# A smaller leading tile, uneven triple tiles, and weight sums spread over PSUM and GpSimd in a two-convolution transducer kernel

## The chip, the cores and the metric

The kernel runs on one core of one Trainium2 chip. The metric is the device time of one execution in microseconds (us), lower is better. Engines are written as the profile writes them: PE is TensorE (PEld its weight loads), DVE is VectorE, ACT is ScalarE, POOL is GpSimd, SP is SyncE, which issues the DMAs here.

## The reference

```
x (2, 4000, 512), w1, w2 (5, 512, 512), g (2, 8, 512), w_f, w_g, w_o (512, 512), all bf16
h  = gelu(conv(x, w1, 5 taps, pad 2))[:, ::2]        # (2, 2000, 512)
f  = gelu(conv(h, w2, 5 taps, pad 2))[:, ::2]        # (2, 1000, 512)
fe = f @ w_f ;  ge = g @ w_g                         # (2, 1000, 512), (2, 8, 512)
j  = tanh(fe[:, :, None, :] + ge[:, None, :, :])     # (2, 1000, 8, 512)
out = j @ w_o                                        # (2, 1000, 8, 512)
```

The convolutions contract 512 channels for each of 5 taps; only every second output is kept, so only those are computed.

## The kernel before, in words

**Order.** A class `Plan` records every operation once, and a table `ORDER` holds, for each engine, the written-out sequence in which that engine gets its operations (each pair of characters is the number of one operation in the order of recording). Semaphore waits are added from the cells that operations read and write. An engine works strictly in its sequence: when its next operation waits, everything behind it waits too. Helpers (`memset`, `tt` for a tensor_tensor, `stt` for a scalar_tensor_tensor, `act` for an activation, `mm` for a matmul over four slices of 128 channels) record the operations, so most of the profile's rows carry the line of a helper: L398 is `tt`, L404 `act`, L412 `mm`.

**The start.** DVE sets a tile `zero` (L419). PE runs eight warming matmuls of 512 columns on it (`warm_mm`, L480 to L486). POOL makes the identity from it (L422). The first rows of x come straight by two DMAs (`load_xr`, 128 rows and 78 rows). PE transposes them in 32 steps against the identity (`turn`, L489), 16 for each load, and ACT and DVE copy the turned rows from PSUM to `xs[0]` (DVE: L505). The taps of w1 come in the order 0, 4, 2, 1, 3 on SP (`load_w1`): taps 0 and 4 in two halves each.

**The leading tile.** The first 408 outputs of h (2 x `NA`, `NA` = 204) of the first batch are computed tap by tap: `direct`, 5 taps x 4 slices of channels x 4 blocks of outputs, 80 matmuls of 408 columns, taps in the order 0, 4, 2, 1, 3.

**The triple tiles.** The other outputs of both convolutions come in `Triple` tiles, where nine matrix products do the work of fifteen. A tile has six phases of x (every sixth row, turned by a transposing DMA on SP: `load_xq` into `xq0`, `xq1`, later `xp2`, `xp0`; phases in the order 4, 0, 2, 1, 3, 5). ACT and DVE form sums and differences of phases in steps (`step`: d0 to d2 scale by 2, r0 to r2, t2, tm, sm and so on), written to `row0` and `row1` or back over a phase. For each of four blocks m of outputs a `Unit` runs products over these: t2 first into a PSUM bank, ACT keeps 1.5 times the result (`sd`), then tm and sm on top of it, ACT keeps its negative, then t1 and s1, and DVE adds (`acc<-acc,sd`). The rest of the first batch is covered by two tiles of `N3` = 266 and 266 columns, the second batch and the second convolution by tiles of 334.

**The weight sums.** The products need sums of taps: `w1part(m)`, for each block m of 128 outputs. With t = w0 + w4: v = t - w2 (a third of it goes to `w1_x[0]`), u = 4 w4 + w0 + 2 w2 (a third goes to `w1_x[1]`), and t + w2 goes to `w1_t[2]`. From taps 1 and 3: 2 w1 (`w1_t[1]`), w1 + w3 (`w1_t[0]`), w1 - w3 (`w1_x[2]`). DVE makes the sums in SBUF buffers (`ssum`, fp32), ACT the scaled copies.

**Later stages.** fe and the joint output use products over sums as well (`Feature`, `Seven`): sums of tanh outputs (`ss<-jT`, L903, on DVE and POOL), evictions of PSUM (`sn<-acc`, L834 on ACT and L835 on DVE), sums over these (`og<-acc,sn`) and stores. These come in the same number before and after; the table `ORDER` says which engine does which.

Of the kernel before, what the change touches and what calls it, by code (L numbers as in the profile page):

```python
# [8 lines left out]
ALU = mybir.AluOpType  # L9
# [54 lines left out]
class Op:  # L64
# [6 lines left out]
        "0Y0Z0a0b0c0d0e0f0g0i0k0l0n0q0y0z0_0-101112131415161718191A1B1C1D1E1F1G1H1p2L2l321I1J2v2S2T1r1s2w2n2N2o2O34352y2V2z2W"  # L71
        "3F3G3C3D392s3X2t3A3Y3Q3S3g3T403a3b3q4A3n3i3r3j3d4J423e4T4B434U3o473t4L4j4M4D3u484E4h4W4Q4k4R5U4X4u4r4x4s4o524z4p4_4v"
        "5e55565y535f586667595W5X5b5c6U5_6W5h6e6X5-6f6u6h6i6364695i6-726b6c6w6A736x707H7a7J7K7y7R7k7O7l7S7h7U7P757V7i7c867d7_"
        "7-767n8c8C897o8A8M87838N8J848e8K8f8E8F8v8_8w8m8n989990918j8P958k8Q9B8x8y9M9O8p9P8q9T9U969Z9a9c9C9o9x9d9W9z9X9qA5ACA2"
        "ABA4A99sAWAGAI9tArAsANAKB3B4BAAiAQAjATBBARAUBMAlAmBeBNAoApBfBtAyAzBGBhBiA-BTBUB0BDBHBEBJCABzBaBKBbBWBXCBBkBlCQCHB_CI"
        "CNBnC0COC1BqBoCKBrCLCuCcC6CdCRCfCvCgCTCjCkC7CxCyCUDODSDBDCDTC_DeDEC-DFCnCoD1DVD2DWDfDYDKDZDlDoDLDpDmDwE1E2D4E4E5D5Db"
        "DcDxDsDtENE7E8EOEKEDEEEiEAEjEBELEcEXEYEdF7ETEoFLEUF0EfElFMEgF1F8FXEmFDFOFfF3FBFPFgFsF4F_G4F-FRFiG5FZFjFSFUFVG1G2GNGG"
        "GHGTGUFoFpFuGAGWG7G8GZGXGJGKGOGaGnGoGcGqGrGhGfHCGwGxH0GdHEH3H1HVH4H9HWHAHbHhH6I4I5HKHNHcHLH7HOHjHpHqHeHYHZHfHRHSIAI7"
        "I8IKHyHzHsIhIbIBILHtIcIiIDJ4J5INIOIRIeISIEIkJKIrIsIfJAJBIlJLJDI_J7IuIvJXI-J8JdJaJbJYJEJgJeJRJNJhK0K1JnJoJSJqJwJOKGK6"
        "JrK3K4KHKbJxK7KVKWK9KcKAKYKZL0KeKfKlKmKNL1KOKJKuL6KKKoL7LZKpL3LTL9KvLGLULaLHLALcL4LyLNLsLjLOLkLtLzLdLJLKLWM2LXM3MCMR"  # L80
        "L-M0MSMuMDMvLmLnM5MJM6MhMiMKMFMUMXMGMVMYMaMxMyMbM_N1M-NPN8N9MoMkNQMpN2MlNBNCNFNGNSNTNYNuNvO1ONNZOONfNgNiNjNVNWN_O2Nx"
        "NyN-O8OdNmOeNnO9OwOTOWOUOxOqOrOXOBOQOCOtOROFOkOuOGP4OzP5OgPBPCOlOhP7O_PHPIPKP8PLPiQ9PjPQPRPNPOQAPXPYPaPrPoPpPbPsPlPm"
        "PyPePfPzQMP-Q0Q3Q4QNQCQDQIQJQFQGQPQQQTQUQXQYQbQeQfQi"),
    "act": (
        "080h0m1U0r1x1W1a1z1Z251Y2b1q271K2m1L2M1-1j2U1t2x1l1M1O332d2R1N3E2g2f2X2u2_3Z3B3H3R2h3h413c2r3K3s3M4K3x3f4C4V3p3y3w38"
        "494F4b3m3W3v4i5V5D464t4Y4P4S4y4d5C574q4w5z5B4n6E5A5g5154685d6V6g786j6v6G6M6a5j65795S6B5a745T627I7A7b6d7s5x7z7T717N6_"
        "7W7j7m5q6T7Q5w778D8d7u7g828O8B886s6t7p6S8X8-8L858o8Y9A8W9G8I8R8i8l9N7G948r9I976m9b9V9D9e9S8z9p9_9rA69YAcAXA8AFAtAdAP"
        "AfAMAeAhASAnBOAVB8BuB9AgBgCFCECs9wB7CGCqB-CJC2CCCrCDCeCwChDQCtDPDRFJDDD-CpE0DGDgEaDnFHCXEbE3D6FxFFFGFID_FwEMEFEZEPGS"
        "FyEpFNF2FYFKG_FCF5FhFzIWFkG-GIGVFvI0IVJ2GpGRGgGsHDJVH2J_HXI2IYHMHPI6I1IXIaJ-IMICIjJ6IdJ3ItI3IZJMIwJWJZK_JfK2JpKTJsNN"
        "KILSKdKRK-KnL2KUKyKqLwL8LVLILRLlL_NqKSLxM4MTMEMwMtMjMHKzMQNsN0MPMmNDNLNRMsOPNhNwNXNkNtNMOfOMNOODNrOpP6OLOiPJOoP9PPPZ"  # L90
        "PkQBPcPqP_Q1QOQHQRQgQdQk"),
    "dve": (
        "000j0o0p1R1S1v1T1V1X231w1u212Z1_1y24221b2a261d1c1Q1e1g1f1P1h1i1k28202p1m2P2Y362c1n2Q2q372e1o302i2k2j2-3U3I3V313J3L3k"
        "3P3z3l3O3N4H3-444I3_4N454Z4l4G4m4a4O4c4-4f4e504g5m5E5G5F5k5Y6D6J6F6C5l5Z5P6Y6l6L6K6Z605Q615N5O5t5p6I7C6H7D7Y6y7B5R5u"
        "6z7L7M7Z6P7q5o7X6Q5r7E6k5s5v7r7e6N806O7t7f6R816p7v6n7w6o6q7x6r8G7F8H8b8g8Z8h8u928t939H8a9F9h9f9Q9l9j9R9g8s9k9J9E9i9n"
        "9y9K9-A09mADA3A7AAA1AEAJ9uAHAOAL9vB5B69LAkAYAZBPAbAuBQAvBCAqA_BjBVBIBFBvB1BYBcBmBLByCaBpCMCPBsCZClC8CzCbCVDUCSD0CWD8"
        "DkDXEyEGEzEHD3DqDMDaE6DdDyDuEqDzEtErGCE9EkECEeEvFbEwEVEhEnFEF9FQExGjFtG6G0FTFaFWG3FqGBG9GYGLGbGPGiHHIGHlHIGyGeHFH5Hi"
        "HBHdH8HkHrHaHgHTI9H_HuIHIoJGIPIFITIgJHIpImJCJ9J0JcJFJjKDJkJiJPJTK5JyKXK8KBKaKgKPKLKjKkLDM8KwLbLfM9L5LBLPLuLYLLM1LeLo"
        "M7MAMBMdN4MLMZMWMzNAMqMcNHNUN3OZNdNbO4NcO5NaO3NzNoOAOVO0OsOSOyOvOHOmPDOYO-PMP2PTPuP3PUPvPSPnPgPtQ5QEQKQVQZQcQj"),
    "pool": (  # L100
        "01020304050s0t0u2A0v0w0x295n8VAaBSAwBRAxBwCYDjBxD9D7DhDiE-DAE_EJEsEIFcEuFeGkFdGlGDHGGFGEHmIIGmHoHJHnJIInIqIJJJKCJlKF"
        "KhKEJmLCKiLFLgLELiLhMfMeN5MgN6N7NeO6O7OaOcObP0P1PWPVPwPx"),
    "sp": (
        "0607090A0B0C0D0E0F0G0H0I0J0K0L0M0N0O0P0Q0R0S0T0U0V0W0X2B2C2D2E2F2G2H2I2J2K5H5I5J5K5L5M8S8T8UB2BZBdC3C4C5C9CiCmDHDIDJ"
        "DNDrDvEQERESEWF6FAFlFmFnFrGMGQGtGuGvGzHQHUHvHwHxH-IQIUIxIyIzJ1JQJUJtJuJvJzKMKQKrKsKtKxLMLQLpLqLrLvMIMMMNMOMnMrNENINJ"
        "NKNlNpOEOIOJOKOjOnPAPEPFPGPdPhQ2Q6Q7Q8QLQSQWQaQh"),
# [3 lines left out]
class Plan:  # L110
# [25 lines left out]
    def dma(self, eng, fn, reads=(), writes=(), sem=None, nbytes=524288, rate=320e3):  # L136

        o = Op()
        o.eng, o.fn, o.dma, o.signal, o.idx, o.alt, o.port = eng, fn, True, False, len(self.ops), None, False
        o.reads, o.writes, o.cost, o.pin, o.after, o.wire = tuple(reads), tuple(writes), 0.43, True, [], nbytes / rate  # L140
# [144 lines left out]
def bass_standalone__seq2seq_rnn_t_joint__speech_kernel(  # L285
# [25 lines left out]
    NA, N3 = 204, (266, 266)  # L311
# [9 lines left out]
    with ExitStack() as es:  # L321
# [27 lines left out]
        zero = at("zero", [NT], BF16)  # L349
# [5 lines left out]
        xq = [Buf(nc, f"xq{i}", [6, NK, (288, 288)[i]], BF16, v.end - v.bytes) for i, v in enumerate((xs[1], w2_sb))]  # L355
# [52 lines left out]
        def mm(o, pairs, start, stop, check=True):  # L408
# [9 lines left out]
        zv = zero[:]  # L418
        pl.op("dve", lambda e: e.memset(zv.ap, 0.0), (), (zv,))  # L419
# [3 lines left out]
            out=idv.ap, in_=zero[0:P].ap, compare_op=ALU.not_equal, fill=1.0, base=0,  # L423
            pattern=[[-1, P]], channel_multiplier=1), (zero[0:P],), (idv,))
# [15 lines left out]
        def load_x6(buf, b, ph, j0, col, n=336):  # L440
# [4 lines left out]
            return pl.dma("sp", lambda e: e.dma_start_transpose(out=dst.ap, in_=src), (), (dst,), nbytes=n * 2 * D, rate=172e3)  # L445
# [18 lines left out]
        def load_xq(i, ph):  # L464
            o = load_x6(xq[i], 0, ph, 2 * NA // 3 + i * N3[0] - 2, 0, -(-(N3[i] + 3 - i) // 16) * 16)
            if (i, ph) in ((0, 4), (0, 0)):
                o.wire = 1.050 if ph else 2.520
# [768 lines left out]
```

## Time and profile before

| | us |
|---|---|
| device time, median of 3 runs | 248.95 |
| lowest and highest run | 248.75, 248.99 |
| span of the profiled execution, on its one core | 247.2 |
| median of the runs less that span | 1.75 |

| engine | busy us | share of the span | instructions |
|---|---|---|---|
| PE (matmul) | 242.8 | 98% | 1932 |
| PEld (weight load) | 186.1 | 75% | 1932 |
| DVE | 224.8 | 91% | 403 |
| ACT | 210.7 | 85% | 359 |
| POOL | 83.8 | 34% | 90 |

The profile lists the profiled execution by its span alone: from its first instruction to its last. What the device time holds beyond it, some 1.75 us, lies around the program. Times in the profile's rows count from the start of the span. A row of the timeline gives start, length, engine, line, operation and tiles, and in brackets how long the engine was idle and what released it; a run of equal instructions stands as one row with its count, and its length reaches to the end of the last one, which for matmuls is modelled and overlaps the next row. Starts are therefore what the pace is read from.

### The profile page before, as it was taken

Reading aid. Unit: us, or ns where it says so; the run is one execution under the profiler, and the core shown is the slowest. Engines: PE = TensorE matmul, PEld = TensorE weight load, DVE = VectorE, ACT = ScalarE, POOL = GpSimd, SP = SyncE. Lnnn points to the kernel's source line nnn. Section 1 sums busy time; section 2 is a strip of 40 time slices with the busy share of each in tenths; the row PEclk is TensorE's granted clock in tenths of the full one; section 3 lists DMA queues with packets and bytes.
Section 4 is the critical chain, followed back from the end, with each engine's and each line's share of the span. In section 5 each row is a group of like instructions: output and inputs, shape, how many; then the busy total and the mean of one; then the engine's idle time right before and its main releaser. Section 6 shows DMA issues by size and latency. Waiting matters only on the chain.

```text
span 247.2 us, 5277 instructions
## 1 busy us (share of the span) xinstructions
PE 242.8 (98%) x1932; PEld 186.1 (75%) x1932; DVE 224.8 (91%) x403; ACT 210.7 (85%) x359; POOL 83.8 (34%) x90
## 2 busy tenths in 40 slices
PE   8999999999999999999999999999999999999995
PEld 4657888877666666666567888778788888888883
DVE  1799998867999999699998999999999999999994
ACT  3269799899669857986799999999999999999992
POOL 1000000000000000000015584677887886796861
PEclk9999999999999999999999999999999999999999
DMA  6998999997700340000000234413433655356377
GB/s 215 331 193 168 185 157 205 150 177 174 254 2 3 119 135 3 1 1 3 0 0 3 85 102 139 143 48 129 131 127 103 195 171 172 132 187 200 123 258 233
DMA packets 57890, 31.87 MB, mean 129 GB/s; under 512 B 33835, under 2 KB 57659, under 8 KB 57865
## 3 DMA queue, kind: packets, MB, share of 16 engines
q1 hardware_dynamic: 57577, 31.41, 48.5%
q8 instruction: 15, 0.25, 0.4%
q10 hardware_dynamic: 288, 0.13, 0.2%
q14 instruction: 10, 0.08, 0.1%
HBM read 7.66 MB, written 16.38 MB: 97 GB/s over the span
## 4 chain that ended last, share of the span: by engine, by line
PE 98%; DVE 0%; issue 0%
PE acc L412 97%; PE acc L496 1%; DVE ost L835 0%; DVE xs L505 0%; DVE zero L419 0%
## 5 line engine op out<-in xcount | busy, mean ns | idle before, releaser
L398 DVE TENSOR_TENSOR og<-acc,sn 128x512 bf16<-128x512 f32 x93 | 60.0, 690 | 1.9 <-PE acc L412 1.2
L412 PE MATMUL acc<-tw,ss 128*128 128x256 f16 x372 | 58.0, 273 | 0.0
L404 ACT ACTIVATE jT<-feT,geT 128x1000 bf16<-128x1000 f32 (+6 forms) x56 | 53.2, 1002 | 1.8 <-DVE feT L398 1.5
L834 ACT ACTIVATE sn<-acc 128x512 f32<-128x512 f32 (+1 forms) x70 | 43.0, 707 | 1.0 <-PE acc L412 0.7
L412 PEld LDWEIGHTS acc<-tw,ss 128*128 128x128 f16 x372 | 36.0, 98 | 6.5 <-ACT sn L834 0.2
L903 POOL TENSOR_TENSOR ss<-jT 128x512 f16<-128x512 bf16 x24 | 27.7, 1168 | 25.0 <-DVE feT L398 22.5
L412 PE MATMUL acc<-row,w_sb 128*128 128x334 bf16 (+1 forms) x192 | 31.7, 296 | 0.0
L412 PE MATMUL acc<-wo_sb,jT 128*128 128x256 bf16 x176 | 29.2, 273 | 0.0
L404 ACT ACTIVATE sd<-acc 128x334 f32<-128x334 f32 (+1 forms) x48 | 20.6, 435 | 10.1 <-PE acc L412 9.6
L412 PE MATMUL acc<-row,w_x 128*128 128x266 bf16 (+1 forms) x192 | 28.4, 291 | 0.0
L404 ACT ACTIVATE jX<-feT,geT 128x1000 bf16<-128x1000 f32 (+4 forms) x28 | 27.4, 1042 | 0.0
L394 POOL MEMSET hT<- 128x8 bf16 (+2 forms) x6 | 0.7, 149 | 70.5 <-ACT hT L404 70.5
L412 PEld LDWEIGHTS acc<-row,w_sb 128*128 128x128 bf16 x192 | 18.7, 98 | 6.3
L412 PEld LDWEIGHTS acc<-row,w_x 128*128 128x128 bf16 x192 | 18.7, 98 | 5.7
L903 POOL TENSOR_TENSOR ss<-jT,ss 128x512 f16<-128x512 bf16 x14 | 16.6, 1189 | 15.1 <-DVE ss L903 9.7
L412 PE MATMUL acc<-wo_sb,ss 128*128 128x256 bf16 x124 | 21.0, 273 | 0.0
L412 PEld LDWEIGHTS acc<-wo_sb,jT 128*128 128x128 bf16 x176 | 17.2, 98 | 3.1
L835 DVE COPY sn<-acc 128x512 f32<-128x512 f32 (+1 forms) x25 | 16.8, 691 | 1.1 <-PE acc L412 1.0
L412 PE MATMUL acc<-hT,w_sb 128*128 128x334 bf16 x96 | 17.1, 305 | 0.0
L518 DVE SCALAR_TENSOR_TENSOR acc<-acc,sd 128x334 f32<-128x334 f32 (+1 forms) x24 | 11.7, 487 | 5.8 <-PE acc L412 5.6
L404 ACT ACTIVATE hT<-acc 128x266 bf16<-128x266 f32 (+2 forms) x36 | 14.6, 433 | 2.7 <-PE acc L412 2.4
L834 ACT ACTIVATE og<-acc 128x512 bf16<-128x512 f32 x22 | 15.3, 710 | 1.5 <-PE acc L412 1.5
(113 smaller groups left out, 502.5 us busy)
## 6 DMA issues: line engine op xcount, KB each, us to landing
out_dram<-og SPq DMA_DIRECT2D x45, 256.0 KB, 2.3
w_sb<-in_w_dram SPq DMA_DIRECT2D x8, 512.0 KB, 4.9
out_dram<-og SPq DMA_DIRECT2D x19, 128.0 KB, 2.2
w_sb<-in_w_dram SPq DMA_DIRECT2D x4, 256.0 KB, 4.8
xr<-in_x_dram SPq DMA_DIRECT2D x1, 512.0 KB, 3.5
wf_sb<-in_w_f_dram SPq DMA_DIRECT2D x1, 512.0 KB, 3.6
wg_sb<-in_w_g_dram SPq DMA_DIRECT2D x1, 512.0 KB, 5.1
wo_sb<-in_w_o_dram SPq DMA_DIRECT2D x1, 512.0 KB, 5.2
```

The source lines that it names most:

```text
L394: pl.op("pool", lambda e: e.memset(v.ap, 0.0), (), (v,))
L398: pl.op(eng, lambda e: e.tensor_tensor(out=o.ap, in0=a.ap, in1=b.ap, op=op), (a, b), (o,), 0.02 + 2.14e-3 * o.ap.free_size() if eng == "po ...
L404: pl.op("act", lambda e: e.activation(o.ap, i.ap, func, scale=scale, bias=0.0 if bias is None else bias.ap), rd, (o,), o.ap.free_size() * ...
L412: ins = e.matmul(o.ap, lhsT=l.ap, rhs=r.ap, start=start and n == 0, stop=stop and n == len(pairs) - 1, skip_group_check=not check)
L496: ins = e.transpose(pv.ap[:, i, k, :], xr[rt].h[0:n, 2 * r + pp, k, :], ident.h[0:n, 0:n])
L518: pl.op(eng, lambda e: e.scalar_tensor_tensor(out=o.ap, in0=a.ap, scalar=f, in1=b.ap, op0=ALU.mult, op1=add), (a, b), (o,), vec_cost(o, (a ...
L834: pl.flex({"act": (lambda e: e.activation(o.ap, v.ap, ACT.Copy), 0.05 + n * 0.833e-3), "dve": (lambda e: e.tensor_copy(out=o.ap, in_=v.ap) ...
L835: "dve": (lambda e: e.tensor_copy(out=o.ap, in_=v.ap), 0.065 + n * 1.04e-3)}, (v,), (o,))
L903: fn = lambda e, o=S[i], x=x, y=y, op=op: e.tensor_tensor(out=o.ap, in0=x.ap, in1=y.ap, op=op)
```

## The change

- `NA` goes from 204 to 192 and `N3` from (266, 266) to (206, 334): the direct tile has 384 columns, the second load of x rows 66 rows, the first triple tile 206 columns and the second 334. Phases of `xq0` are loaded with 224 rows each instead of 272, those of `xq1` with 336 instead of 272.
- The tile `zero` is gone. The warming matmuls read a bf16 constant 1.0, the identity is made from an fp32 constant 0.
- On SP tap 3 is issued behind phases 4 and 0 of `xq0` (before: ahead of all phases).
- `w1part`: ACT copies w4 to a PSUM bank for every block m, and u is built there by DVE. For m = 0 and 1 t and v lie in PSUM too. For m = 2 and 3 POOL makes t, v and `w1_t[2]` in SBUF, six tensor_tensor operations of 128x512.
- `scaled` lets a scaling copy go to ACT or DVE; `shared` does so for the sums of taps 1 and 3 (DVE or POOL). The operations of the direct tile are no longer pinned to their place ahead of the triple products: its last 16 matmuls stand between the first two triple products.
- The memsets at the edge of `xq1` are split, one for each phase, on POOL.
- The whole table `ORDER` is new. The number of matmuls is the same (1932). Over the whole kernel nine sums `ss` go from DVE to POOL, six evictions `sn` from ACT to DVE, some sixteen scaling steps from ACT to DVE, and the eviction of the last half tile from DVE to ACT.

The order of the first instructions of PE after the change: 8 warming matmuls, transposes, 64 direct matmuls, 4 of the first triple product (t2, m = 0), 8 direct on tap 3, 4 of t2, 8 direct on tap 3, 4 of t2, then the products tm and sm, all of 206 columns.

```diff
-    NA, N3 = 204, (266, 266)
+    NA, N3 = 192, (206, 334)
...
-        zero = at("zero", [NT], BF16)
...
-        xq = [Buf(nc, f"xq{i}", [6, NK, (288, 288)[i]], BF16, v.end - v.bytes) for i, v in enumerate((xs[1], w2_sb))]
+        xq = [Buf(nc, f"xq{i}", [6, NK, (352, 352)[i]], BF16, v.end - v.bytes) for i, v in enumerate((xs[1], w2_sb))]
...
-        zv = zero[:]
-        pl.op("dve", lambda e: e.memset(zv.ap, 0.0), (), (zv,))
...
-            out=idv.ap, in_=zero[0:P].ap, compare_op=ALU.not_equal, fill=1.0, base=0,
+            out=idv.ap, in_=nc.const_aps.tensor(0.0, [P, P], FP32), compare_op=ALU.not_equal, fill=1.0, base=0,
...
         lo, hi, al = slice(0, 2), slice(2, NK), slice(0, D)
         for i, part, gate in ((0, (lo, al), None), (0, (hi, al), None), (4, (slice(0, NK), slice(0, D // 2)), None),
-                              (4, (slice(0, NK), slice(D // 2, D)), 0), (2, None, 1), (1, None, 3), (3, None, 5)):
+                              (4, (slice(0, NK), slice(D // 2, D)), 0), (2, None, 1)):
             load_w1(i, part, gate)
-        for ph in (4, 0, 2, 1, 3, 5):
-            load_xq(0, ph)
+        for kind, i in (('w', 1), ('x', 4), ('x', 0), ('w', 3), ('x', 2), ('x', 1), ('x', 3), ('x', 5)):
+            if kind == "w":
+                load_w1(i, None, len(came) - 4)
+            else:
+                load_xq(0, i)
...
         def warm_mm(n):
-            o, z, zz = ps.cols(3 * NT, NT), zero[0:P], zero[:]
+            o = ps.cols(3 * NT, NT)
+            one = [nc.const_aps.tensor(1.0, [P, k], BF16) for k in (P, NT)]
             for _ in range(n):
-                mm(o, [(z, zz)], True, True)
+                pl.op("pe", lambda e: e.matmul(o.ap, lhsT=one[0], rhs=one[1], start=True, stop=True), (), (o,))
...
+        WBANK = ((6, 7), (5, 4), (6, 7), (5, 4))
+        WHOME = ('P', 'P', 'G', 'G')
...
         def w1part(m, part):
             sl = slice(m * P, (m + 1) * P)
             w = lambda i: w1_sb[i, :, sl]
-            if part == "s":
-                t, v, u = ssum[4][:], ssum[m % 2][:], ssum[2 + m % 2][:]
...
-                tt("dve", t, w(0), w(4), add)
-                stt("dve", u, w(4), 4.0, w(0))
-                stt("dve", u, w(2), 2.0, u)
-                act(w1_x[1, :, sl], u, ACT.Copy, scale=1.0 / 3.0)
+            home = WHOME[m]
+            if home != "S":
+                u, t = (ps.cols(bk * NT, NT).map(lambda a: a.rearrange("p (k c) -> p k c", k=NK)) for bk in WBANK[m])
+                act(u, w(4), ACT.Copy)
+                w4 = u
...
+            if home == "G":
+                t, v = ssum[4][:], ssum[m % 2][:]
+                tt("pool", t, w(0), w(4), add)
+                tt("pool", v, t, w(2), sub)
+                tt("pool", w1_t[2, :, sl], t, w(2), add)
+            else:
+                v = t if home == "P" else ssum[m % 2][:]
+                tt("dve", t, w4, w(0), add)
+            stt("dve", u, w4, 4.0, w(0))
+            stt("dve", u, w(2), 2.0, u)
+            act(w1_x[1, :, sl], u, ACT.Copy, scale=1.0 / 3.0)
+            if home != "G":
+                tt("dve", w1_t[2, :, sl], t, w(2), add)
                 tt("dve", v, t, w(2), sub)
-                act(w1_x[0, :, sl], v, ACT.Copy, scale=1.0 / 3.0)
-                tt("dve", w1_t[2, :, sl], t, w(2), add)
+            act(w1_x[0, :, sl], v, ACT.Copy, scale=1.0 / 3.0)
...
-        memset(xq[1][0:4, :, 1 + N3[1]:4 + N3[1]])
-        memset(xq[1][4:6, :, N3[1]:4 + N3[1]])
+        for ph in (4, 0, 2, 1, 3, 5):
+            memset(xq[1][ph, :, (1 if ph < 4 else 0) + N3[1]:4 + N3[1]])
...
+        pl.pin = False
         for i in taps:
...
-        w1part(0, "s")
+        for m in range(NK):
+            w1part(m, "s")
+        for m in (0, 2):
+            w13part(m)
```

More of the change, by code (lines that the diff above doesn't have):

```diff
@@ L139, in dma @@
         o.eng, o.fn, o.dma, o.signal, o.idx, o.alt, o.port = eng, fn, True, False, len(self.ops), None, False
-        o.reads, o.writes, o.cost, o.pin, o.after, o.wire = tuple(reads), tuple(writes), 0.43, True, [], nbytes / rate
+        o.reads, o.writes, o.cost, o.pin, o.after, o.wire = tuple(reads), tuple(writes), 0.43, not reads, [], nbytes / rate
         if sem is None:
@@ L497, in fn @@
                 return ins
-            pl.op("pe", fn, (xr[rt].rows(0, n), ident[:]), (pv,), k * (0.2 if rt else 0.275))
+            pl.op("pe", fn, (xr[rt].rows(0, n), ident[:]), (pv,), k * 4 * (n / 128) * (0.06 if rt else 0.08))
             o = xs[0][pp::2, :, 16 + rt * P:16 + rt * P + n] if k == 2 else xs[0][2 * rs[0] + pp:2 * rs[0] + pp + 1, :, 16 + rt * P:16 + rt * P + n]
@@ L538, in w2part, with scaled @@
                 act(w(1), w(1), ACT.Copy, scale=2.0)
-        w13 = {0: 2, 2: 4}
+        WBANK = ((6, 7), (5, 4), (6, 7), (5, 4))
+        WHOME = ('P', 'P', 'G', 'G')
+        def scaled(o, i, f):
+            n = o.ap.free_size()
+            fast = not i.psum and o.ap.dtype == BF16 and i.ap.dtype == BF16
+            pl.port = fast
+            pl.flex({"act": (lambda e: e.activation(o.ap, i.ap, ACT.Copy, scale=f), n * 0.833e-3 + (0.05 if i.psum else 0.105)),
+                     "dve": (lambda e: e.tensor_scalar_mul(out=o.ap, in0=i.ap, scalar1=f), 0.065 + n * (0.26e-3 if fast else 1.04e-3))}, (i,), (o,))
+            pl.port = False
         def w1part(m, part):
@@ L560, in bass_standalone__seq2seq_rnn_t_joint__speech_kernel, with shared @@
+        def shared(o, x, y, op, pool):
+            pl.port = True
+            fn = lambda e: e.tensor_tensor(out=o.ap, in0=x.ap, in1=y.ap, op=op)
+            n = o.ap.free_size()
+            pl.flex({"dve": (fn, 0.065 + 0.52e-3 * n), **({"pool": (fn, 0.02 + 2.14e-3 * n)} if pool else {})}, (x, y), (o,))
+            pl.port = False
         banks, later = [4, 5, 6, 7, 3], [0, 1, 2]
@@ L625, in s1 @@
                 self.t.product("t2", self.m, self.A, True)
-                act(self.c, self.pa(), ACT.Copy, scale=1.5)
+                scaled(self.c, self.pa(), 1.5)
             def s2(self):
@@ L630, in s2 @@
                 self.t.product("sm", self.m, self.A, False)
-                act(self.s, self.pa(), ACT.Copy, scale=-1.0)
+                scaled(self.s, self.pa(), -1.0)
             def s3(self):
@@ L780, in steps @@
             when(slot, *[lambda w=w: trip[i].step(w) for w in STEPS[lo:hi]])
-        w1part(0, "s")
+        for m in range(NK):
+            w1part(m, "s")
+        for m in (0, 2):
+            w13part(m)
         for w in STEPS:
             trip[0].step(w)
-        for m in range(1, NK):
-            when((0, 0, 1)[m - 1], lambda m=m: w1part(m, "s"))
         when(17, load_late, lambda: tail_zero(1))
```

97 lines of the change are left out of this document (46 added, 51 removed).

## The prediction

> **What bounds the kernel now.** I read the head of the page first, then the chain of work that ended last, by engine and by line.
>
> ```profile
> span 247.2 us, 5277 instructions
> PE 242.8 (98%) x1932; PEld 186.1 (75%) x1932; DVE 224.8 (91%) x403; ACT 210.7 (85%) x359; POOL 83.8 (34%) x90
> ...
> PE 98%; DVE 0%; issue 0%
> PE acc L412 97%; PE acc L496 1%; DVE ost L835 0%; DVE xs L505 0%; DVE zero L419 0%
> ```
>
> TensorE (PE) is busy for 98% of the span and makes 98% of the chain. The same chain in order of time (start, duration, what) shows where it is not PE:
>
> ```profile
> 0.86 0.28 DVE zero L419
> 1.14 0.05 issue
> 1.19 3.59 PE acc L412 x8
> 4.78 2.18 PE acc L496 x24
> 6.96 0.02 issue
> 6.99 0.33 DVE xs L505
> 7.32 0.05 issue
> 7.37 236.76 PE acc L412 x1892
> ```
>
> From 7.37 to 244.13 us one piece of 1892 matmuls runs without a break that counts. So only three things can move the time: what lies ahead of 7.37, the columns that PE streams behind it, and waits that the new order puts into that piece. VectorE (DVE) with 91% and ScalarE (ACT) with 85% are near enough to full that such waits are the main doubt. The profiled execution has a span of 247.2 us; the median of the three runs is 248.95, so 1.75 us lie around the span, and I keep them as they are. The sum is made against the span and carried to the median unchanged.
>
> **The start.** The timeline of the first microseconds:
>
> ```profile
> 0.31 0.10 POOL L1221 MEMSET const-bfloat16-1.0<- 128x1 bf16 x1
> 4.27 0.10 PEld L496 LDWEIGHTS acc<-ident,xr 128*128 128x128 bf16 x1 [0.40 <-DMA xr<-in_x_dram]
> 4.58 2.66 PE L496 MATMUL acc<-ident,xr 128*128 128x128 bf16 x32
> 5.67 0.42 DVE L505 COPY xs<-acc 128x512 bf16<-128x512 bf16 x1 [4.54 <-PE acc L496]
> ```
>
> The eight warming matmuls go from 1.19 to 4.58, 0.424 us each. They wait for the memset of zero, which ends at 1.14. The constant that replaces it is there at 0.41, so the run can begin when the engines begin, about 0.8, and ends about 4.2. The rows of x have landed by 4.27, so the first transpose moves from 4.58 to about 4.28: 0.30 us. Then the landing is the late one, and nothing more is to be had here. The chain needs 24 transposes before the last copy: 16 of 128 columns and 8 of 78, which become 8 of 66. They took 2.38 us (4.58 to 6.96) for 2672 columns, 0.89 ns a column; 96 columns fewer save 0.09. The copy shrinks from 312 to 264 columns; from 0.42 at 512 and 0.33 at 312 that is 0.45 ns a column, 0.02. Sum: -0.41 us, and the direct matmuls begin at about 6.96. The identity is made from a constant too, and is ready earlier than its use at 4.27.
>
> **The columns.** The timeline of PE, where one kind of matmul follows another:
>
> ```profile
> 7.37 12.65 PE L412 MATMUL acc<-xs,w_sb 128*128 128x408 bf16 x72
> 19.86 1.98 PE L412 MATMUL acc<-row,w_x 128*128 128x266 bf16 x16
> ...
> 23.05 2.88 PE L412 MATMUL acc<-row,w_x 128*128 128x266 bf16 x24
> 25.77 2.88 PE L412 MATMUL acc<-xq,w_t 128*128 128x266 bf16 x24
> ```
>
> Start to start, 72 matmuls of 408 columns took 12.49 us, 173.5 ns each; 24 of 266 took 2.72, 113.3 ns each: 0.424 ns per column over 142 columns. The direct tile has 80 matmuls, each 24 columns shorter: -1920 columns. A triple tile has 144 matmuls; the two tiles go from 266+266 to 206+334 columns: +1152. The number of matmuls stays at 1932. Net -768 columns, at 0.424 ns: **-0.33 us**.
>
> For the 206-column matmuls the same slope gives 87.9 ns. That is only so if the weights of the next one load behind it:
>
> ```profile
> L412 PEld LDWEIGHTS acc<-row,w_sb 128*128 128x128 bf16 x192 | 18.7, 98 | 6.3
> ...
> 108.35 0.39 PEld L412 LDWEIGHTS acc<-gT,wg_sb 128*128 128x128 bf16 x8
> ```
>
> The first row (a group: busy, mean ns of one) shows 98 ns from start to end of a load, longer than 87.9. But the second shows eight loads of the same size within 0.39 us, 49 ns each: loads overlap. So I take 87.9, nearest to the second row, and keep 98 as the other end: 144 x (98 - 87.9) = 1.5 us. The Trainium skill ("TensorE: Matmul & The Clock Gate", LDWEIGHTS) has a load take its 128 columns divided by 1.2, some 107 ns; by that rule the 206-column matmuls would cost 144 x 19 = 2.7 us more and the change would be a loss of 2. The eight loads in 0.39 us speak against it as a limit on the pace.
>
> **The transfers.** Tap 3 now goes behind two turned phases. Answers for the DMA issues in three stretches (8.7 to 9.0: tap 3; 9.2 to 9.4: phase 4; 10.95 to 11.3: phase 0) give microseconds from issue to landing, and a row of GpSimd (POOL) shows the end of the last phase of xq1:
>
> ```profile
> DMA packets 107, 0.11 MB, mean 365 GB/s; under 512 B 0, under 2 KB 107, under 8 KB 107
> w_sb<-in_w_dram SPq DMA_DIRECT2D x1, 512.0 KB, 4.8
> xq<-in_x_dram SPq DMA_TRANSPOSE x1, 5.4
> xq<-in_x_dram SPq DMA_TRANSPOSE x1, 6.1
> 32.09 0.12 POOL L394 MEMSET xq<- 128x32 bf16 x1 [1.12 <-DMA xq<-in_x_dram]
> ```
>
> So tap 3 landed at 13.6, phase 4 at 14.6 (1.0 later), phase 0 at 17.1 (2.45 later). A tap of 0.524 MB at 365 GB/s is 1.44 us; a phase of 224 rows, not 272, takes 0.82 of its time. Estimate for the new order: phase 4 at 13.0, phase 0 at 15.0, tap 3 at 16.4. PE comes to tap 3 after 64 direct matmuls and 4 of the first triple product: 6.96 + 64 x 0.1633 + 4 x 0.088 = 17.8. That covers it by 1.4 us; if transposed phases hold the queue longer than I think, each microsecond over 1.4 is lost in full. The four phases after it come later by tap 3's 1.44, less what shorter phases save. For all twelve phases 3264 rows become 3360, so the last lands at about 32.09 + 0.03 x 18.5 = 32.6, and xq1's phase 0, four phases of 1.9 us ahead of that, at about 25. POOL's second memset waits for it, and behind that in POOL's order stands the last of its weight sums (w1_t[2] for the last quarter).
>
> **The weight sums and the row combinations.** Durations from the timeline of DVE (the next start gives the pace), groups of ACT and POOL, and the stretch 20 to 35 (PE, PEld, DVE, ACT, POOL busy):
>
> ```profile
> 18.00 0.72 DVE L398 TENSOR_TENSOR row<-xq 128x1064 bf16<-128x1064 bf16 x1
> 18.62 0.69 DVE L518 SCALAR_TENSOR_TENSOR ssum<-w_sb,ssum 128x512 f32<-128x512 bf16 x1
> 19.22 0.69 DVE L398 TENSOR_TENSOR ssum<-ssum,w_sb 128x512 f32<-128x512 f32 x1
> ...
> 27.33 0.44 DVE L518 SCALAR_TENSOR_TENSOR acc<-acc,sd 128x266 f32<-128x266 f32 x1
> 27.68 0.71 DVE L398 TENSOR_TENSOR row<-row 128x1064 bf16<-128x1064 bf16 x1
> L404 ACT ACTIVATE w_x<-ssum 128x512 bf16<-128x512 f32 x8 | 4.9, 623 | 7.5 <-DVE ssum L518 5.5 <-DVE ssum L398 2.0
> L903 POOL TENSOR_TENSOR ss<-jT 128x512 f16<-128x512 bf16 x24 | 27.7, 1168 | 25.0 <-DVE feT L398 22.5
> 20.00:35.00 15.00, 15.00 (x131) 12.48 (x129) 14.99 (x28) 12.67 (x25) 0.57 (x5) 1.00 1.03 170
> ```
>
> DVE is full there (14.99 of 15), ACT has 2.3 us free, POOL nearly all. Six sums of 128x512 leave DVE: 6 x 0.60 = 3.6 us. They cost POOL 6 x 1.17 = 7.0; the first five run from 9 to about 15.5. The last starts at about 25 and ends at 26.4; PE reads it at about 28.4. ACT gains four copies to PSUM, 4 x 0.62 = 2.5 us, within its free time. Nothing in before shows DVE adding from PSUM to PSUM at this size; the nearest row is 0.69 for 512 columns, and the accumulator row of 0.44 for 266 with 0.35 to the next one bounds it: 0.55 to 0.70 each. Fourteen such are DVE's; eleven lie ahead of phase 0's landing, so between -0.5 and +1.1 us. I take 0.60: 6.6 us from about 8.5, done just as phase 0 lands.
>
> The tight place is 20 to 27 us. Behind phase 0's landing at 15.0 DVE has 23 instructions until the sum that frees the accumulator PE wants in its sixtieth step: 11 row combinations of 824 elements at 0.50 (from 0.62 at 1064), 7 of 512 to 1024 at 0.60, 5 of 206 at about 0.32. That is 11.3, to 26.3, and about 0.9 of waiting for ACT and PE: 27.2. PE needs it at 6.96 + 80 x 0.1633 + 84 x 0.088 = 27.4. Five steps between 21 and 27 have only 0.1 to 0.3 us of cover by the same count, so I put +0.1 for waits, with 0 and +1.0 as ends.
>
> **Behind 35 us** the set of products is the same, in a new order. Nine sums go from DVE to POOL, six evictions from ACT to DVE, some sixteen scaling steps from ACT to DVE. The stretch 150 to 200:
>
> ```profile
> 150.00:200.00 50.00, 50.00 (x420) 40.53 (x419) 48.97 (x93) 49.70 (x79) 35.16 (x32) 1.00 0.38 124
> ```
>
> PE is busy all of it, with DVE at 48.97, ACT at 49.70 and POOL at 35.16. PE has nothing to gain; what the moves may do is delay it. I take nothing, with up to two POOL sums (2.3 us) as the other end. The last accumulator half is evicted by ACT in place of DVE: even, within 0.05.
>
> **Sum.** 248.95 - 0.41 - 0.33 + 0.1 = **248.3 us**.
>
> **Rivals.** *Tight waits.* Several of the five steps come late, or warming begins no earlier than 1.19 because the engine's own start is the later one: +0.2 to +0.9, so 248.5 to 249.2. For it: DVE full in 20 to 35. Against: it sheds 3.6 us of sums there. Chance 0.23.
>
> *Slower by the late sums.* In the joint stage a sum that POOL makes in 1.17 us (a DVE operation takes 0.60) is the last thing that PE waits for. Its place is 140 to 200 us, where DVE and ACT leave 1.0 and 0.3 us of 50. Each sum late by its full length costs 1.17; from the first one on, the gain of 0.65 is gone and the time is 249.5, with two 250.6. For it: nine more sums on POOL. Against: POOL has 14.8 us free of those 50. Chance 0.16.
>
> *The clock.* The warming matmuls run at 0.83 ns a column, the direct ones at 0.424, so the clock doubled between 4.58 and 7.37. The change moves the warming by 0.4 and the direct tile by 0.41 together. If the doubling is not moved with them, direct matmuls that begin ahead of it run at half pace, and each microsecond of that costs half; one warming run's length late (3.4 us) gives +1.7, 250.0. Against: in before the direct tile was at full pace at once. Chance 0.08. The Trainium skill (the same page, "What's actually happening") calls the window free-running, about 3.4 us; no run shown here tells its phase, and it would give the same 1.7.
>
> *Weight loads limit the 206-column matmuls.* +1.5, so 249.8. Against: the 49 ns loads. Chance 0.04.
>
> *More gain.* Small gaps that before has in its long piece close, or PSUM sums go faster: 247.8 to 248.1. Chance 0.04.
>
> **The numbers.** The forecast of 248.2 to 248.5 has 0.45. About 0.2%, 0.5 us, is what a measurement can tell from no change, so faster is below 248.45 and slower above 249.45. Faster: 0.42 of the forecast, 0.04 and 0.01 of the tight waits, 0.47. Same: 0.03 and 0.20, 0.23. Slower: 0.02, 0.16, 0.08, 0.04, 0.30. The range 247.8 to 250.0 leaves out most of the late sums and part of the clock's case. The likeliest case alone is 248.2 to 248.5.
>
> **What would show it.** Right: the first warming matmul below 0.9, the first transpose at 4.3, direct matmuls from 6.95 at 163 ns, 206-column ones at 88 ns, tap 3 landed before 17.8, the PE piece again unbroken and its end near 243.5. Wrong: a gap of PE at 20 to 28 behind DVE or ACT, direct matmuls at 326 ns, or PE waiting for POOL behind 140.

## The result and the profile after

The changed kernel takes 250.21 us (median of six runs, 249.62 to 250.84). The kernel before takes 248.89 beside it (six runs, 248.75 to 249.05). The ratio is 1.0053, with a 95% interval of 1.0042 to 1.0064: slower by half a per cent, where 248.3 was forecast. Its runs spread over 1.2 us, those of the kernel before over 0.3.

The head of the page and the chain that ended last, by engine:

```profile
span 248.3 us, 5283 instructions
PE 242.6 (98%) x1932; PEld 183.6 (74%) x1932; DVE 228.6 (92%) x406; ACT 200.7 (81%) x343; POOL 101.6 (41%) x110
...
PE 73%; DVE 8%; ACT 7%; DMA 4%; issue 4%; SPq 1%; DVEq 0%; ACTq 0%
```

PE's share of the chain has fallen from 98% to 73%. DVE, ACT and, new, DMAs are in it. The same chain in order of time shows where:

```profile
6.55 152.87 PE acc L410 x1162
...
176.77 4.22 DMA out_dram<-og
181.11 0.69 DVE og L396
182.32 0.72 DVE feT L396
...
209.00 2.13 DMA out_dram<-og
...
214.99 29.61 PE acc L410 x268
```

Up to 159.4 PE runs as one piece. Then the chain goes through DVE and ACT, twice through a store that had to land before DVE could write to an output buffer, and back to PE at 215. PE's last piece ends at 244.60; before, it ended at 244.13. So PE ends 0.47 later, although it begins its direct matmuls 0.82 earlier (6.55 against 7.37) and streams fewer columns. From there to the end of the span it is 3.7 us, where it was 3.07. Together that is the 1.1 us by which the span grew (247.2 to 248.3).

The timeline of PE at the start and in the first tiles:

```profile
0.78 3.57 PE L483 MATMUL acc<-const-bfloat16-1.0 128*128 128x512 bf16 x8 [0.78 <-PEq L1246]
4.14 1.92 PE L496 MATMUL acc<-ident,xr 128*128 128x128 bf16 x32
...
6.55 10.60 PE L410 MATMUL acc<-xs,w_sb 128*128 128x384 bf16 x64 [0.49 <-DMA w_sb<-in_w_dram]
16.99 0.52 PE L410 MATMUL acc<-row,w_x 128*128 128x206 bf16 x4
...
23.13 2.28 PE L410 MATMUL acc<-xq,w_t 128*128 128x206 bf16 x24
25.25 0.87 PE L410 MATMUL acc<-row,w_x 128*128 128x206 bf16 x8
```

Warming begins at 0.78, and the 32 transposes take 1.92 us where they took 2.66. Then PE waits 0.49 us for the weights of tap 0, which it did not before. Start to start, 64 matmuls of 384 columns took 10.44 us, 163.1 ns each; 24 of 206 took 2.12, 88.3 ns each.

The late stages. First what the engines waited for from 150 us on (us in total, times, the longest). Before:

```profile
DVE og L398 <- DMA out_dram<-og: 0.3, 1, 0.3
```

After:

```profile
DVE og L396 <- DMA out_dram<-og: 1.6, 4, 0.7
PEld acc L410 <- DVE sn L867: 1.3, 4, 0.5
PEld acc L410 <- DVE og L396: 1.3, 5, 0.4
PEld acc L410 <- DVE feT L396: 0.7, 1, 0.7
```

Then the busy time in two stretches (PE, PEld, DVE, ACT, POOL, with the number of instructions; behind them the granted clock, the share of the DMA engines and GB/s). Before:

```profile
180.00:190.00 10.00, 10.00 (x89) 8.39 (x87) 10.00 (x18) 10.00 (x16) 9.07 (x8) 1.00 0.34 112
210.00:220.00 10.00, 10.00 (x93) 8.68 (x92) 9.72 (x19) 10.00 (x18) 8.03 (x8) 1.00 0.58 185
```

After:

```profile
180.00:190.00 10.00, 9.61 (x82) 7.57 (x81) 9.56 (x18) 9.72 (x16) 8.64 (x9) 1.00 0.28 89
210.00:220.00 10.00, 9.75 (x84) 7.59 (x83) 9.44 (x19) 9.41 (x16) 6.42 (x6) 1.00 0.53 169
```

DVE waits 1.6 us for stores out of `og` (0.3 before), and PE's weight loads then wait for DVE. The counts in the stretches say it too: 82 and 84 matmuls where there were 89 and 93. Measured from start to start against their normal pace, PE's matmuls lose 2.1 us between 182 and 216, where those of the kernel before lose 0.1. No POOL row stands among what PE waits for.

### The profile page after: what moved, and what is told of

Same layout as the page of the kernel before. It is cut to its first block, busy times and chain, and to the rows that moved or that the text cites. A ratio compares the mean times of both kernels' runs of the same rounds, so it can differ in the third digit from the quotient of the medians.

```text
span 248.3 us, 5283 instructions
## 1 busy us (share of the span) xinstructions
PE 242.6 (98%) x1932; PEld 183.6 (74%) x1932; DVE 228.6 (92%) x406; ACT 200.7 (81%) x343; POOL 101.6 (41%) x110
## 4 chain that ended last, share of the span: by engine, by line
PE 73%; DVE 8%; ACT 7%; DMA 4%; issue 4%; SPq 1%; DVEq 0%; ACTq 0%
PE acc L410 73%; DVE og L396 3%; ACT jX L402 3%; DMA out_dram<-og 3%; DMA w_sb<-in_w_dram 2%; ACT sn L866 2%; DVE sn L867 2%; ACT og L866 1%; ACT jT L402 1%; DVE feT L396 1%; DVE og L867 1%; SPq L983 1%; DVE ss L935 1%; DVE sn L871 0%; SPq L434 0%
## 5 line engine op out<-in xcount | busy, mean ns | idle before, releaser
L402 ACT ACTIVATE jT<-feT,geT 128x1000 bf16<-128x1000 f32 (+6 forms) x56 | 50.8, 952 | 0.8 <-DVE feT L867 0.6
L866 ACT ACTIVATE sn<-acc 128x512 f32<-128x512 f32 (+1 forms) x63 | 36.1, 608 | 4.3 <-PE acc L410 3.9
L410 PE MATMUL acc<-row,w_x 128*128 128x334 bf16 (+1 forms) x192 | 29.4, 292 | 0.0
L547 ACT ACTIVATE sd<-acc 128x334 f32<-128x334 f32 (+1 forms) x40 | 16.9, 428 | 11.2 <-PE acc L410 10.6
L402 ACT ACTIVATE jX<-feT,geT 128x1000 bf16<-128x1000 f32 (+4 forms) x28 | 24.9, 929 | 0.0
L935 POOL TENSOR_TENSOR ss<-ss,jT 128x512 f16<-128x512 f16 x16 | 18.5, 1164 | 8.6 <-DVE ss L935 8.5
L867 DVE COPY sn<-acc 128x512 f32<-128x512 f32 (+1 forms) x32 | 21.1, 682 | 0.6 <-PE acc L410 0.5
L402 ACT ACTIVATE hT<-acc 128x334 bf16<-128x334 f32 (+2 forms) x36 | 14.6, 436 | 7.1 <-PE acc L410 6.9
L410 PE MATMUL acc<-row,w_t 128*128 128x334 bf16 x96 | 16.5, 305 | 0.0
L410 PE MATMUL acc<-xp,w_t 128*128 128x334 bf16 x96 | 16.2, 304 | 0.0
```

What stands on the lines that cost most here:

```text
L402: pl.op("act", lambda e: e.activation(o.ap, i.ap, func, scale=scale, bias=0.0 if bias is None else bias.ap), rd, (o,), o.ap.free_size() * ...
L410: ins = e.matmul(o.ap, lhsT=l.ap, rhs=r.ap, start=start and n == 0, stop=stop and n == len(pairs) - 1, skip_group_check=not check)
L547: pl.flex({"act": (lambda e: e.activation(o.ap, i.ap, ACT.Copy, scale=f), n * 0.833e-3 + (0.05 if i.psum else 0.105)), "dve": (lambda e: e ...
L866: pl.flex({"act": (lambda e: e.activation(o.ap, v.ap, ACT.Copy), 0.05 + n * 0.833e-3), "dve": (lambda e: e.tensor_copy(out=o.ap, in_=v.ap) ...
L867: "dve": (lambda e: e.tensor_copy(out=o.ap, in_=v.ap), 0.065 + n * 1.04e-3)}, (v,), (o,))
L935: fn = lambda e, o=S[i], x=x, y=y, op=op: e.tensor_tensor(out=o.ap, in0=x.ap, in1=y.ap, op=op)
```

## The experiments

Two kinds of edits come back below. "The order of the kernel before from PE's operation n on" means: every operation that PE's first n operations need keeps its place, and the rest follows in the sequence of the kernel before, on every engine:

```
ORDER[e] = [i for i in changed[e] if i in needed] + [i for i in before[e] if i not in needed]
```

With the sequence, the choice of engine for each later operation goes back too. The place where the two orders meet is called the cut or the seam.

A further buffer for `og` lies in the space of `fT0`, which is free by then. Where PE "loses", that is the time from one matmul's start to the next, less the usual time for that number of columns.

**The old late order under the new front.** Edit: the line above with n = 232.

> The changed kernel, with the order of all engines taken from the kernel before from PE's operation 232 on (about 119 us of the span, behind the first convolution's triple tiles); start, leading tile, weight sums and first tiles stay as changed. Theory A, the loss lies in the new order of the late stages alone: start -0.82 and columns -0.33 stay, the 2.1 us of waits between 180 and 216 and the 0.6 us longer end go, so about 247.8 us. Rival B, the late waits follow from the front (everything runs earlier and meets other transfers, or buffers come free at other times): the waits stay under the old order too, 249.5 to 250.2 us.

Measured: 248.85 us, ratio to the kernel before 1.0001 (0.9988 to 1.0015). That is 1.4 below the changed kernel, and no loss between 180 and 216 is left:

```profile
180.00:190.00 10.00, 10.00 (x88) 8.23 (x86) 10.00 (x19) 10.00 (x17) 9.09 (x8) 1.00 0.35 114
210.00:220.00 10.00, 10.00 (x93) 8.70 (x91) 9.89 (x19) 10.00 (x18) 8.15 (x8) 1.00 0.54 174
```

So the front does not cause the late waits; Rival B falls. But 247.8 was expected. The profile has two losses that are not the theory's. One is the seam: PE waits for ScalarE at 121, 0.7 us against its pace. The other is new, at 26 to 28 us, again 0.7, and the timelines of POOL and DVE show what lies under it:

```profile
24.80 1.20 POOL L403 TENSOR_TENSOR w_t<-ssum,w_sb 128x512 bf16<-128x512 f32 x1
```

```profile
24.62 0.37 DVE L555 TENSOR_SCALAR xq<-row 128x824 bf16<-128x824 bf16 x1
25.02 1.42 DVE L403 TENSOR_TENSOR row<-row 128x824 bf16<-128x824 bf16 x1
```

DVE's operation took 1.42 us. In the profile of the changed kernel the same two lie the other way round, and it took 0.59, while POOL's sum took 1.29:

```profile
25.29 1.29 POOL L396 TENSOR_TENSOR w_t<-ssum,w_sb 128x512 bf16<-128x512 f32 x1
```

```profile
24.58 0.37 DVE L548 TENSOR_SCALAR xq<-row 128x824 bf16<-128x824 bf16 x1
24.98 0.59 DVE L396 TENSOR_TENSOR row<-row 128x824 bf16<-128x824 bf16 x1
25.49 0.37 DVE L396 TENSOR_TENSOR sd<-acc,sd 128x206 f32<-128x206 f32 x1
```

Whichever begins first keeps its length; the other is drawn out. In the first pair DVE's operation ends 0.44 us behind the end of POOL's sum. The Trainium skill ("SBUF — State Buffer", SBUF: two separate sides) says just this: GpSimd and VectorE share a pair of SBUF ports, held for a whole instruction, and an operation of VectorE with two SBUF inputs needs it. The 1.42 us agree. The other weight sums of POOL (9 to 15.4 us) lie beside DVE operations that read PSUM; there all of DVE's take 0.68 or 0.69 and POOL's 1.15 to 1.17.

**A fourth output buffer.**

```diff
+        og.append(at("og3", [4, NT], BF16, jT.end))
```

> The changed kernel with a fourth output buffer og (in the space of fT0, free by then), nothing else. Theory A1, the late waits come from og buffers that are not free because their stores have not landed (DVE waits 1.6 us for out_dram<-og): these waits go and PE's waits behind 180 shrink by 1.0 to 1.6, so 248.6 to 249.2 us. Rival A2, DVE is late in that order by its own work and the stores are only the last of several reasons: other releasers take the place, 249.9 to 250.2 us.

Measured: 250.42 us, ratio 1.0057 (1.0039 to 1.0076). The time does not fall. In the profile DVE's waits for stores go from 1.6 to 1.0 and PE's loss between 182 and 216 from 2.1 to 1.4, but this execution had the collision at 25 us (0.7). That would explain the median only if most of the six executions had it, and only the profiled one is seen. Not decided by itself; the same edit with two buffers follows.

**The warming alone, in the kernel before.**

```diff
-                mm(o, [(z, zz)], True, True)
+                pl.op("pe", lambda e: e.matmul(o.ap, lhsT=one[0], rhs=one[1], start=True, stop=True), (), (o,))
```

> The kernel before, with the warming matmuls reading the constant 1.0 and the identity made from the constant 0; the memset of zero stays but nobody waits for it. By the prediction's own count the start gains 0.30: direct matmuls from about 7.07, 248.6 us. Theory C, the granted clock moves with the warming by more than its own 0.4 us, so the transposes run at full pace as they do in the changed kernel (56 ns per 128 columns): transposes end near 6.0, direct matmuls from 6.4 to 6.7 (then the weights of tap 0 are the late ones), 248.1 to 248.3 us.

Measured: 248.90 us, ratio 1.0002 (0.9989 to 1.0014): nothing, neither 248.6 nor less. In its profile warming starts at 0.77, but the rows of x landed late in that execution:

```profile
4.96 1.96 PE L497 MATMUL acc<-ident,xr 128*128 128x128 bf16 x32 [0.61 <-DMA xr<-in_x_dram]
7.06 0.33 PE L412 MATMUL acc<-xs,w_sb 128*128 128x408 bf16 x1
```

The transposes took 1.96 us, as after the change, and direct matmuls began 0.31 earlier than before. PE lost 0.3 again at 23.5 and 28.2, waiting for rows that DVE forms no earlier than before (0.1 later at 23, at the same time at 28). In this profile, then, a start gained without earlier data is given back at the first tile that needs them. The weights, too, landed 0.1 to 0.5 later in this execution, so it is no clean test.

**The old end.** Edit: the cut with n = 700.

> The changed kernel, with the order of all engines taken from the kernel before from PE's operation 700 on (the last 5 us of matmuls): the last full og blocks go to ACT and the last half tiles to DVE again. Theory A: the end from the last matmul to the last landing shrinks from 4.0 to 3.4 us, 249.6 us. Rival: the end is set by the stores' own time whatever engine evicts, 250.2 us.

Measured: 250.73 us, ratio 1.0073 (1.0055 to 1.0090). The miss has a reason that is not the theory's: behind the cut PE loses 1.05 us at 239.7 to 244.6, waiting for DVE at the seam. This execution also had a collision at 25 us (0.6). From its last matmul's start to the end of the span the profile has 3.35 us, against 3.99 for the changed kernel and 3.36 before. So the end itself is as the theory says, the time is not; inconclusive as a price.

**POOL's last weight sum kept apart, and forced to collide.** Two kernels. In the first, one dependency is added; in the second the sum stands ahead of the two edge memsets in POOL's order, behind an earlier operation of DVE.

```diff
+        pl.ops[118].after.append(143)     # w1_t[2], last block, behind DVE's row0[0]
```

```diff
+        pl.ops[118].after.append(141)     # behind DVE's xq0[2]
```

> The changed kernel with one wait more: POOL's last weight sum (w1_t[2], last block) starts only when DVE has formed row0[0] (at about 25.6), so that it runs beside DVE operations that read PSUM. Theory L, the sum of POOL and a DVE operation with two SBUF inputs shut each other out: in three of four profiles of this front the sum began at 24.4 to 24.8 and a DVE operation of 0.37 or 0.59 us took 1.05 or 1.42, and PE then lost 0.6 to 0.7 us at 26 to 28; kept apart, no DVE operation there takes longer and the median falls by 0.4 to 0.6, to about 249.7. Rival M, those 0.7 us come from tight waits on DVE and ACT in general (the prediction's rival): no change, 250.2 us.

> The changed kernel with POOL's last weight sum made to start at about 24.4, ahead of the two edge memsets and behind DVE's xq0[2], so that it always lies beside DVE's single-input copy and row0[0]. Theory L: one of these two takes about 0.7 to 0.8 us longer in every execution, PE loses 0.6 to 0.7 at 26 to 28, median 250.3 to 250.6, about 0.7 above the kernel that keeps them apart. Rival M: the same time as the kernel that keeps them apart.

Measured: 250.24 us kept apart (ratio 1.0063, 1.0049 to 1.0076) and 251.35 colliding (1.0104, 1.0086 to 1.0121). The collision costs 1.1 us, somewhat more than expected; in the profiles PE loses 1.0 at 20 to 30 where it loses 0.1 with the sum kept apart. Here it is a copy with a single SBUF input that waits:

```profile
24.80 1.16 POOL L401 TENSOR_TENSOR w_t<-ssum,w_sb 128x512 bf16<-128x512 f32 x1 [9.27 <-DVE xq L401]
```

```profile
24.92 1.47 DVE L553 TENSOR_SCALAR xq<-row 128x824 bf16<-128x824 bf16 x1
```

Kept apart, the sum begins 0.84 later, and the copy takes its usual time:

```profile
25.64 1.16 POOL L396 TENSOR_TENSOR w_t<-ssum,w_sb 128x512 bf16<-128x512 f32 x1
```

```profile
24.57 0.37 DVE L548 TENSOR_SCALAR xq<-row 128x824 bf16<-128x824 bf16 x1
```

Rival M falls: with the same front and 0.84 us between two places of one POOL sum, the loss at 26 to 28 is there or not. But keeping them apart did not lower the median of the changed kernel (250.24 against 250.21), where 0.4 to 0.6 was expected. So theory L holds for the mechanism and fails for its weight: the collision is not what makes the changed kernel slow. How often the two meet is not settled. Of the five profiles below and above that leave the sum free, four have a DVE operation drawn out (the old late order, four buffers, the old end, five buffers); that of the changed kernel has none.

**Five output buffers.**

```diff
+        og += [at(f"og{i}", [4, NT], BF16, jT.end + (i - 3) * 4096) for i in (3, 4)]
```

Three kernels have it: the changed one with the sum kept apart, the changed one as it is, and the kernel before.

> As the one before, and five output buffers og (two more, in the space of fT0). Theory A1, stores that have not landed hold DVE up in the new late order (1.6 us of waits with three buffers, 1.0 with four): the rest of it goes too, PE's waits behind 180 fall from 2.1 to below 1, so 1.0 to 1.3 us below the run before it in this list. Rival A2, DVE and ACT are late there by their own chain: at most 0.3 below it.

> The changed kernel with five output buffers og, without the extra wait for POOL's last weight sum. Theory A1: about 1.5 below the changed kernel, 248.7 us. What it tells beside that: if the sum meets a DVE operation in most executions (theory L as first put), it is 0.4 to 1.0 above the kernel with both (248.7), if seldom, the same.

> The kernel before, with five output buffers og instead of three, nothing else. Theory A1 says that the buffers are short only in the new late order (before, a tile holds its buffer 5.3 us and the next user comes 5.2 us later on average; changed, 6.8 and 4.2): no change within 0.3, 248.6 to 248.9 us. Rival: stores hold both kernels up alike, 247.5 to 248.2 us.

Measured: 248.72 us with the sum kept apart (ratio 1.0000, 0.9992 to 1.0009), 248.79 without (1.0006, 0.9995 to 1.0017), and 248.89 for the kernel before (1.0011, 0.9996 to 1.0027). Two more buffers take 1.4 to 1.5 us off the changed kernel and nothing off the kernel before. DVE's waits for stores are gone from the list of waits, and the stretches with them:

```profile
180.00:190.00 10.00, 10.00 (x87) 7.98 (x86) 10.00 (x19) 10.00 (x16) 9.19 (x9) 1.00 0.37 120
210.00:220.00 10.00, 10.00 (x94) 8.96 (x93) 9.95 (x21) 10.00 (x19) 7.11 (x7) 1.00 0.65 211
```

PE's loss between 182 and 216 is 0.5, down from 2.1. Theory A1 holds: it is the new order that needs more buffers. Matching DVE's and ACT's rows one by one with the written-out order tells why. A tile of the joint stage writes its `og` buffer in four blocks. From the start of the first to the end of the last of them it took 5.3 us on average before and 6.8 in the changed kernel, so from the last block to the next user of the same buffer 5.2 us were left before and 4.2 now, at the least 1.7 and 1.0. A store of 256 KB takes about 2.3 us to land.

The second kernel also weighs the collision. Its profiled execution had it:

```profile
25.21 1.16 POOL L398 TENSOR_TENSOR w_t<-ssum,w_sb 128x512 bf16<-128x512 f32 x1
```

```profile
25.29 1.53 DVE L398 TENSOR_TENSOR row<-row 128x824 bf16<-128x824 bf16 x1
```

That execution took 249.61 us. But it has a second loss, 0.4 us at 20.5, ahead of the collision's 0.8; both stand in PE's timeline:

```profile
20.99 2.63 PE L412 MATMUL acc<-row,w_x 128*128 128x206 bf16 x28 [0.24 <-DVE row L398]
...
26.87 0.53 PE L412 MATMUL acc<-row,w_sb 128*128 128x206 bf16 x4 [0.43 <-DVE row L398]
```

Of this kernel's eleven executions, seven lie between 248.46 and 248.85, one at 249.0 and three between 249.6 and 249.8; with the sum kept apart all eleven lie between 248.41 and 249.17. That fits a loss of some 0.9 us at the front in about a quarter of the executions, by a collision in part or in whole. Only the profiled one is seen.

**The old late order, seam mended, sum kept apart.** Edit: n = 232, two products of the second convolution behind two feature products on PE, and the dependency from above.

> The order of the kernel before from PE's operation 232 on, as in the first run of the study, with the seam mended (two products of the second convolution go behind two feature products, so that PE does not wait 0.7 us at 121 for ScalarE) and POOL's last weight sum kept apart. Theory A with L: what is left is the start (-0.7), the columns (-0.33) and no loss, so 247.5 to 247.8 us, faster than both kernels. Rival B (the late stage takes the gain back wherever it comes from): 248.6 to 248.9 us.

Measured: 248.37 us, ratio 0.9984 (0.9974 to 0.9994): below both kernels, by 0.4 us and by 1.8, and between what theory and rival gave. In the profile PE loses 0.3 at the seam still, and direct matmuls begin at 6.82 rather than 6.55, since tap 0 landed at 6.58 in that execution. The span is 246.6, 0.6 less than before: 0.55 of the start and 0.3 of the columns, less 0.25 of waits.

**The warming late again.** The kernel of the last paragraph, where the first warming matmul waits for the identity.

> The kernel with the old late order and the sum kept apart (248.4 us), where the first warming matmul waits for POOL's identity, so that it starts at about 1.25 and not 0.77, as late as in the kernel before. If the earlier start reaches the end: direct matmuls from about 7.0 to 7.1 in place of 6.5 to 6.8, 0.3 to 0.5 above, 248.7 to 248.9. Rival: PE meets the same data at 20 to 28 us whenever it starts and gives the time back there: 248.3 to 248.5.

Measured: 248.75 us, ratio 0.9999 (0.9987 to 1.0011), 0.38 above the kernel without the wait, but the two intervals overlap, and the profiles do not differ at the place: warming at 1.28, direct matmuls at 6.80 (6.82 there), span 246.7 (246.6 there).

```profile
1.28 3.60 PE L490 MATMUL acc<-const-bfloat16-1.0 128*128 128x512 bf16 x8 [1.28 <-POOL xs L399]
...
6.80 0.65 PE L417 MATMUL acc<-xs,w_sb 128*128 128x384 bf16 x3 [0.16 <-DVE xs L512]
```

Inconclusive on what the earlier warming is worth at the end.

**Five buffers and the old end.** Edit: five `og`, the sum kept apart, the cut with n = 710.

> Five og, POOL's last weight sum kept apart, and the order of the kernel before from PE's operation 710 on (the last 3 us of matmuls). The changed end puts two stores of 256 KB behind 243 us and takes 4.0 us from the last matmul to the end, against 3.4 before. Theory A: 0.5 to 0.6 below the kernel without it, 248.1 us, below the kernel before. Rival: the stores that wait at the end are those of the tiles before the cut, so the end stays at 4.0, 248.7 us.

Measured: 250.06 us, ratio 1.0057 (1.0045 to 1.0069). The cut costs 0.9 us at 241.2, where PE waits for ScalarE, and the end stays at 4.2 us from the start of the last matmul, although DVE evicts the last half tiles again: the large stores are those of tiles ahead of the cut, as the rival says. Its profile also has what the prediction held covered, tap 3 late:

```profile
16.87 0.52 PE L417 MATMUL acc<-row,w_x 128*128 128x206 bf16 x4
17.97 1.47 PE L417 MATMUL acc<-xs,w_sb 128*128 128x384 bf16 x8 [0.59 <-DMA w_sb<-in_w_dram]
```

## Why the prediction was wrong, point by point

**The step that failed** is "Behind 35 us": "I take nothing, with up to two POOL sums (2.3 us) as the other end." There lie 2.1 us of waits between 182 and 216. The size was inside the bound, the mechanism was not. I asked only whether nine more sums make POOL late. No POOL sum is what PE waits for; DVE waits for output buffers whose stores have not landed. I had counted how many operations each engine does and not how far apart the order puts the four blocks of one tile. That could have been read from the two orders beside the trace of before, where the shortest time between a buffer's last block and its next user was already 1.7 us. The chance of 0.16 for a loss in the late stage was too small: DVE and ACT left 1.0 and 0.3 us of 50, which I quoted, and that is little slack for a whole new order.

**The end** was taken as "even, within 0.05" for one eviction that changes engine. It cost 0.6 to 0.7. The engine that evicts is not what matters: with five buffers and the old end DVE evicts again, and the end stays long. What differs is the stores. The last rows of the DMA queue, before and after:

```profile
242.50 0.39 SPq L951 DMA_DIRECT2D out_dram<-og  x1
243.04 1.67 SPq L959 DMA_DIRECT2D out_dram<-og  x3
```

```profile
243.36 1.00 SPq L983 DMA_DIRECT2D out_dram<-og  x2
244.40 1.25 SPq L991 DMA_DIRECT2D out_dram<-og  x2
```

Lines L951 and L983 are the stores of 256 KB. Before, the last one goes out at 242.50, 1.6 us ahead of PE's end, and three halves follow. After, two of them go out from 243.36, so the last halves queue behind them: the last takes 2.8 us from issue to landing where it took 2.0. That kernels with the old end take 3.3 to 3.4 us again (the old late order, and the cut at 700) supports this; no run changed these two stores alone.

**The start** was right in sign and too small: -0.82 in the profile where -0.41 was forecast (6.43 to 6.82 over the profiles of this front). The term mis-sized is the 24 transposes, taken at 0.89 ns a column as before, where the pace doubled behind most of them. The 32 now take 1.92 us. Measured start to start, a transpose of 128 columns takes 107 ns in both profiles with the old warming. In the twelve profiles with the constant most of the 16 take 56 ns in six, some of them in five, none in one, and in one of those with some the warming began as late as 1.28. The granted clock in the profile's rows reads 1.00 in every stretch of the first 8 us; it is the pace of the matmuls that shows the doubling. With warming from 0.77 it came at about 6.0 us in one profile (the collision forced), behind 19 transposes, and at about 3.4 in another (the old late order, sum kept apart), within the warming itself, whose seventh matmul took 280 ns where the second to the sixth took 426 or 427:

```profile
0.77 3.17 PE L490 MATMUL acc<-const-bfloat16-1.0 128*128 128x512 bf16 x8 [0.77 <-PEq L1254]
```

So the place where the pace doubles is not tied to the start of the warming by a fixed time, as I had taken it to be; it moves by some 2.6 us between executions. The Trainium skill ("TensorE: Matmul & The Clock Gate", What's actually happening) has a free-running window, which does not begin anew with the kernel; the profiles agree with that, but the 500 ns that the page gives for the spread is less than is seen here. The clock's rival did not come: no direct matmul ran at half pace. What is late next, which I did not name, is the weights of tap 0, which land at 6.1 to 6.6: in two of the profiles, that of the changed kernel among them, PE waits for them.

**The columns** were right: 163.1 and 88.3 ns measured, 163.3 and 87.9 forecast. The 107 ns that follow for a weight load from the Trainium skill ("TensorE: Matmul & The Clock Gate", LDWEIGHTS) are no limit on the pace here; 24 matmuls, each with its own load, follow each other at 88.3.

**Tap 3** was given 1.4 us of cover. In the profile of the changed kernel PE did not wait, with 0.3 left; in another of the same front it waited 0.59. The estimate of 16.4 was too early: tap 3 landed at 17.0 in the changed kernel, and between 15.4 and 17.9 over the profiles of this front. Phase 0 ahead of it was estimated too late, at 15.0; it landed at 13.4.

**The tight place** at 20 to 27 us held in the profile of the changed kernel, as counted (PE loses 0.05 there). But the count took each DVE operation at the length that it has alone, and left out that a POOL sum in SBUF shuts it out. That costs PE 0.6 to 1.0 us in the profiles where the landing of one phase of `xq1` puts the sum there, and it can make the time of this front uneven.

**The sum**, by the trace: -0.8 for the start, -0.3 for the columns, +1.6 for waits beyond those of before, +0.6 for the end: +1.1, as the spans show. With five output buffers the medians are 248.72 and 248.79: of the 1.9 us by which the forecast of 248.3 was missed, 1.4 to 1.5 were the late waits for stores, and what is left is about the size of the longer end.

## What to carry to other kernels

When an order is written anew for engines that are full, count for each ring of buffers how long one owner holds a buffer and how long until the next one writes, and set that against the landing of the store; the number of operations per engine does not show it. Where GpSimd takes over work, look at what VectorE does in the same microsecond: beside operations that read PSUM the sum was free; beside operations from SBUF to SBUF it drew one out by 0.7 to 1.1 us, up to nearly its own 1.16. And an earlier start is worth only what the data behind it allow; one profile here suggests it, none proves it.

## What the runs showed of the hardware

- PE's pace doubled at a place that differs between executions of the same front, from about 3.4 to about 6.0 us: 16 transposes of 128 columns took 107 ns each in one profile and 56 in others. Transposes do run at the full pace.
- A POOL sum of 128x512 that takes 1.16 us stretched a DVE sum of two SBUF tiles from 0.59 to 1.42 and 1.53, and a DVE copy from SBUF to SBUF from 0.37 to 1.47. When DVE came first, POOL's sum grew to 1.29.
- The same load of 512 KB (tap 3), issued behind two transposing DMAs, landed between 15.4 and 17.9 us in eleven profiles of the same front.
